# Late experts' blocks: partial sums kept in one PSUM bank and read while they grow

## The chip, the cores and the metric

The kernel runs on one core of a Trainium2 chip, as one program. The metric is its device time in microseconds (us), the median over runs; the profile is one further execution, taken with the hardware profiler.

## The reference: what is computed

An attention block without softmax (a state that decays at each step) makes `y` of shape batch 4, heads 8, 768 steps, 48 wide. Laid out as 3072 tokens of 384 numbers it goes into a mixture of 8 experts, two for each token:

```python
for t in range(S):
    state = f[:, :, t, :, None] * state + einsum('bhd,bhe->bhde', k[:, :, t], v[:, :, t])
    y[:, :, t] = einsum('bhd,bhde->bhe', q[:, :, t], state)
x = y.transpose(0, 2, 1, 3).reshape(3072, 384)
noisy = x @ w_gate + log1p(exp(x @ w_noise)) * noise
top2 = argpartition(-noisy, 2, axis=1)[:, :2]; top2_w = softmax over the two
for e in range(8):
    for k in range(2):
        mask = top2[:, k] == e
        h = maximum(x[mask] @ w1[e], 0.0)             # 384 -> 1024
        out[mask] += top2_w[mask, k, None] * (h @ w2[e])   # 1024 -> 384
```

All of it is in 32-bit floating point.

## The kernel before

**Stages.** First come attention and the routing, which write for each expert a list of its tokens; then the experts. A *pair* is 256 tokens of one list (two blocks of 128). An *item* is an expert with one to three pairs. Items 0 to 3 are early ones with one pair each; the twelve items end with eight *late* ones, 4 to 11, which take two or three pairs at once. `late_experts` sets their order: items 4, 5, 10 and 11 have two pairs (a *side* is then 256 tokens wide), items 6 to 9 have three (a side of 384). Tokens over 768 in a list are done in five blocks of 32, the *quarter* blocks, which are woven in among the pieces of items 6 to 10 (`quarter_block`, L1126 to L1161).

**Products saved.** A product of two matrices cut into 2 by 2 blocks is made here of seven block products and not eight: sums of blocks are made first (on VectorE), seven products are taken (on TensorE), and their results are combined. The first layer of a late item (`first_of_two`) does this for two of the three 128-row chunks of `x` and two sides of tokens: `a(half, chunk, j)` is a 128 by 128 block of `w1`, `b(chunk, side)` a chunk of the tokens' features turned round. Sums of `w1` are `s(1)` to `s(5)`, kept in `ws` (tile `v_all`), sums of `b` are `t(1)` to `t(4)`, kept in `ts` (tiles `v_all`, `f_all` and `qk_all`). The third chunk is multiplied plainly. A *group* `j` (four of them in an item) makes the hidden blocks `c(half, side)` of tile `hs_b`: eleven matmul calls of side width, each of which is two instructions in the trace. Calls and their order on TensorE: P1, X twice, P6, V twice, P7, Z twice, W twice, into seven PSUM banks.

The second layer of a pair (`second_layer`, one *call* for a pair, seven *pieces* with a `yield` behind each) does the same with halves of the 1024 hidden features, two blocks of tokens and two halves of the output's columns: seven products of four matmul calls, 192 columns wide. Its sums of hidden blocks are `sm[1]` to `sm[4]` (tile `f_all`, made by `inner_sums`), those of `w2` are `u[1]` to `u[4]` (tile `qk_all`, by `second_sums`). The result is scaled by the gate and added to the output in DRAM by GpSimd's indirect DMA (`scatter`).

**Order.** `in_order` ties each engine's instructions to the order in which the program's text issues them, so an instruction that waits holds up all behind it on its engine. Across engines there are only the waits that data and buffers need. Between the pieces `between` puts in the transposes of the next item's tokens (`turned`) and the sums for the next item's first layer (`first_sums`, L899). `one_bank` hands out the eight PSUM banks in turn. `ahead(1, ...)` and `ahead(2, ...)` put the loads of later weights on SP's queue.

Of the kernel before, what the change touches and what calls it, by code (L numbers as in the profile page):

```python
# [10 lines left out]
F32 = mybir.dt.float32  # L11
# [3 lines left out]
AF = mybir.ActivationFunctionType  # L15
AX = mybir.AxisListType
ALU = mybir.AluOpType
# [314 lines left out]
def kernel(  # L332
# [38 lines left out]
    nc = tc.nc  # L371
    B, H, S, D = q.shape
# [545 lines left out]
    def first_of_two(k):  # L918


        size = side_of(k)
        hs = wide[1][:, :, 0:2 * size]
        w = w1[home(k)]

        def a(half, chunk, j):
            return w[:, chunk, (half * FH + j) * 128:(half * FH + j + 1) * 128]

        def b(chunk, side):
            return (wide[0] if side else xt_a)[:, chunk, 0:size]

        def m(to, x, y, start, stop):
            nc.tensor.matmul(to, lhsT=x, rhs=y, start=start, stop=stop)  # L932

        def t(n):
            return ts[n][:, 0:size]

        for j in range(FH):
            def c(half, side):
                return hs[:, half * FH + j, side * size:(side + 1) * size]

            def s(n):
                return ws[n][:, j * 128:(j + 1) * 128]

            def bank(n):
                return one_bank(f"{n}{k}_{j}")[:, 0:size]

            def add(to, x, y):
                nc.vector.tensor_tensor(to, x, y, ALU.add)  # L948

            one, two, three, both = [kept(size) for _ in range(4)]  # L950
            P1, P6, V, P7, X, Z, W = bank("P1"), bank("P6"), bank("V"), bank("P7"), bank("X"), bank("Z"), bank("W")
            m(P1, a(0, 0, j), b(0, 0), True, True)
            nc.scalar.copy(one, P1)
            m(X, a(0, 1, j), b(1, 0), True, False)
            m(X, a(0, 2, j), b(2, 0), False, True)
            add(c(0, 0), one, X)
            nc.scalar.activation(c(0, 0), c(0, 0), AF.Relu)
            if j == FH - 1:
                inner_sums(hs, 3)
            m(P6, s(2), t(2), True, True)  # L960
            add(two, one, P6)
            m(V, s(1), t(1), True, False)
            m(V, a(1, 2, j), b(2, 1), False, True)
            add(both, two, V)
            m(P7, s(3), t(3), True, True)
            add(three, two, P7)
            add(c(1, 1), three, V)
            nc.scalar.activation(c(1, 1), c(1, 1), AF.Relu)  # L968
            if j < 2:
                second_sums(k, (3, 2)[j])  # L970
            yield
            m(Z, s(4), b(1, 1), True, False)
            m(Z, s(5), b(2, 1), False, True)
            add(c(0, 1), both, Z)
            nc.scalar.activation(c(0, 1), c(0, 1), AF.Relu)
            m(W, a(1, 1, j), t(4), True, False)
            m(W, a(1, 2, j), b(2, 0), False, True)
            add(c(1, 0), three, W)
            nc.scalar.activation(c(1, 0), c(1, 0), AF.Relu)
            if j < 2:  # L980
                second_sums(k, (1, 4)[j])
            if j == FH - 1:
                ahead(1, k + NR + 1)
            yield
        for q in range(len(items[k][1])):
            if q:
                inner_sums(hs[:, :, q * 256:], 3)
            yield from second_layer(k, first_of[k] + q, hs[:, :, q * 256:])

    def inner_sums(hs, which):  # L990
        def a(f, s):
# [3 lines left out]
                    3: (a(0, 0), a(0, 1), ALU.subtract), 4: (a(1, 0), sm[2], ALU.subtract)}[which]  # L995
        nc.vector.tensor_tensor(sm[which], x, y, op)  # L996

    def second_layer(k, p, hs):


        def a(f, s):
            return hs[:, f * FH:(f + 1) * FH, s * 128:(s + 1) * 128]

        def b(f, c):
            return w2[home(k)][:, f * FH:(f + 1) * FH, c * HC:(c + 1) * HC]

        bank, P = [], {}

        def product(name, x, y):
            if name not in (7, 5):  # L1010
                bank.append(one_bank(f"y{p}_{len(bank)}"))
            P[name] = bank[-1][:, HC:DM] if name in (7, 5) else bank[-1][:, 0:HC]
            for o in range(FH):
                nc.tensor.matmul(P[name], lhsT=x[:, o, :], rhs=y[:, o, :], start=(o == 0), stop=(o == FH - 1))  # L1014

        ys = [moved.tile([128, DM], F32, tag=f"ys{s}", name=f"ys{p}_{s}") for s in range(2)]
        P17 = ffn.tile([128, 2, HC], F32, tag="P17", name=f"P17_{p}", bufs=1)
        mid = ffn.tile([128, HC], F32, tag="mid", name=f"mid{p}", bufs=1)

        gate = [slots[p][:, s, 1:2].bitcast(F32) for s in range(2)]  # L1020

        def scatter(s):
            into = nc.gpsimd.indirect_dma_start(out=out, out_offset=bass.IndirectOffsetOnAxis(ap=slots[p][:, s, 2:3], axis=0),  # L1023
                                         in_=ys[s], in_offset=None, bounds_check=N - 1, oob_is_err=False, compute_op=ALU.add)
            tc.declare_no_dep(into.ins, group=f"pair{p}", reason="a list's tokens differ")
            tc.add_to_no_dep_group(f"pair{p}", into.ins)
            if p < NE:
                tc.declare_no_dep(into.ins, group="second half", reason="rows differ")
                tc.add_to_no_dep_group("first half", into.ins)


        calls = first_of[k + 1] - first_of[k]
        q = p - first_of[k]
        last = q == calls - 1
        turns_now, sums_now = {}, {}
        if k + 1 < len(items):
            to_turn = [(to, s) for to in range(first_of[k + 1], first_of[k + 2]) for s in range(2)]
            each = -(-len(to_turn) // calls)
            for piece, to in zip((1, 3) if each == 2 else (1, 2, 3) if each == 3 else (1, 2, 3, 4), to_turn[each * q:each * (q + 1)]):
                turns_now[piece] = [to]  # L1040
        if NE <= k + 1 < len(items):
            if q == 0:
                sums_now = {1: ["w1"], 2: ["w2"], 3: ["w3"], 4: ["w4"], 5: ["w5"]}
            if last:
                most = k + 1 > NE
                sums_now[4] = (["t1", "t2"] if most else []) + sums_now.get(4, [])
                sums_now[5] = (["t3", "t4"] if most else ["t1", "t2", "t3", "t4"]) + sums_now.get(5, [])

        def between(piece):
            for to in turns_now.get(piece, ()):  # L1050
                turned(*to)
            for which in sums_now.get(piece, ()):
                first_sums(k + 1, which)

        left, right = [y[:, 0:HC] for y in ys], [y[:, HC:] for y in ys]
        product(1, a(0, 0), b(0, 0))
        inner_sums(hs, 1)
        yield
        if k >= NE:
            between(1)  # L1060
        product(7, sm[3], u[3])
        nc.scalar.copy(P17.rearrange("t a w -> t (a w)"), bank[0][:, 0:DM])
        nc.scalar.mul(left[0], P17[:, 0], gate[0])
        if k < NE:
            between(1)
        inner_sums(hs, 2)
        yield
        product(4, a(1, 1), u[4])
        inner_sums(hs, 4)
        between(2)  # L1070
        yield
        product(5, sm[1], u[1])
        nc.vector.tensor_tensor(left[1], P17[:, 1], P[4], ALU.add)  # L1073
        nc.vector.tensor_tensor(right[1], P17[:, 1], P[5], ALU.add)
        between(3)
        yield
        product(6, sm[2], u[2])
        nc.vector.tensor_tensor(mid, P17[:, 0], P[6], ALU.add)
        for to in (left[1], right[1]):
            nc.vector.tensor_tensor(to, to, mid, ALU.add)  # L1080
        if p == NP - 1:
            nc.vector.tensor_scalar(ys[1], ys[1], gate[1], None, ALU.mult)
        else:
            nc.scalar.mul(ys[1], ys[1], gate[1])  # L1084
        scatter(1)
        nc.vector.tensor_tensor(mid, mid, P[5], ALU.add)
        nc.scalar.mul(right[0], mid, gate[0])
        between(4)
        yield
        product(2, a(1, 0), b(1, 0))  # L1090
        nc.vector.scalar_tensor_tensor(left[0], in0=P[2], scalar=gate[0], in1=left[0], op0=ALU.mult, op1=ALU.add)
        between(5)
        yield
        product(3, sm[4], b(1, 1))
        if last:
            ahead(2, k + NR + 1)
        nc.vector.scalar_tensor_tensor(right[0], in0=P[3], scalar=gate[0], in1=right[0], op0=ALU.mult, op1=ALU.add)
        scatter(0)
        if p == NP - 3:
            nc.gpsimd.drain()  # L1100
        between(6)
        yield
# [332 lines left out]
```

## Time and profile before

| | us |
|---|---|
| device time, median of 3 runs (range) | 647.41 (647.27 to 647.53) |
| the profiled execution: device time | 648.66 |
| its span, from the first to the last instruction | 646.9 |
| TensorE busy over the span | 635.9 (98%) |
| VectorE (DVE) busy | 443.2 (69%) |
| ScalarE (ACT) busy | 253.9 (39%) |
| GpSimd (POOL) busy | 270.8 (42%) |
| mean granted TensorE clock | 0.996 of full |

The profiled execution is 1.25 us above the median and 1.76 us above its own span. Of the engines TensorE is the fullest. In the profile a matmul's end is modelled, and the next one may start before it, so TensorE's busy share alone doesn't tell whether it waits; the starts of its rows do. PE is TensorE's matmuls and PEld its weight loads.

### The profile page before, as it was taken

Reading aid. Unit: us, or ns where it says so; the run is one execution under the profiler, and the core shown is the slowest. Engines: PE = TensorE matmul, PEld = TensorE weight load, DVE = VectorE, ACT = ScalarE, POOL = GpSimd, SP = SyncE. Lnnn points to the kernel's source line nnn. Section 1 sums busy time; section 2 is a strip of 40 time slices with the busy share of each in tenths; the row PEclk is TensorE's granted clock in tenths of the full one; section 3 lists DMA queues with packets and bytes.
Section 4 is the critical chain, followed back from the end, with each engine's and each line's share of the span. In section 5 each row is a group of like instructions: output and inputs, shape, how many; then the busy total and the mean of one; then the engine's idle time right before and its main releaser. Section 6 shows DMA issues by size and latency. Waiting matters only on the chain.

```text
span 646.9 us, 12901 instructions
## 1 busy us (share of the span) xinstructions
PE 635.9 (98%) x4883; PEld 549.7 (85%) x4883; DVE 443.2 (69%) x993; ACT 253.9 (39%) x602; POOL 270.8 (42%) x301
## 2 busy tenths in 40 slices
PE   8999999999999999999999999999999999999994
PEld 8999999888999999989758965995698579989994
DVE  6777878875656576677757575757566666767862
ACT  6976876752222233233332233323322332232330
POOL 7733899825476530352501460325034213503213
PEclk9999999999999999999999999999999999999998
DMA  9999888889998423368706560926093427622104
GB/s 186 195 224 206 175 166 161 180 213 289 293 246 205 75 42 103 55 193 297 194 27 241 108 186 10 310 38 195 11 311 68 124 88 235 134 64 26 23 1 55
DMA packets 153897, 96.31 MB, mean 149 GB/s; under 512 B 115600, under 2 KB 146320, under 8 KB 153824
## 3 DMA queue, kind: packets, MB, share of 16 engines
q1 hardware_dynamic: 141648, 76.12, 43.4%
q0 software_dynamic: 12176, 19.25, 15.4%
q8 instruction: 41, 0.67, 0.4%
q14 instruction: 32, 0.26, 0.1%
HBM read 75.97 MB, written 19.62 MB: 148 GB/s over the span
## 4 chain that ended last, share of the span: by engine, by line
PE 92%; DMA 3%; POOL 1%; ACT 1%; DVE 1%; SPq 0%; issue 0%; POOLq 0%; ACTq 0%
PE y L1014 34%; PE P L932 8%; PE hp L907 6%; PE X L932 5%; PE V L932 5%; PE Z L932 5%; PE W L932 5%; PE xp L626 3%; PE sc L573 3%; PE y L591 3%; DMA x_rows<-xs 3%; PE xgp L855 2%; PE y L602 1%; PE kp L533 1%; PE qp L533 1%; PE ds L597 1%
## 5 line engine op out<-in xcount | busy, mean ns | idle before, releaser
L1023 POOL DMA_INDIRECT out_dram<-ys,slots x48 | 81.0, 1687 | 160.1 <-ACT ys L1084 131.4
L1014 PE MATMUL y<-qk_all,f_all 128*128 128x192 f32 x576 | 105.3, 327 | 0.0
L1014 PEld LDWEIGHTS y<-qk_all,f_all 128*128 128x128 f32 x576 | 93.3, 190 | 0.4 <-DVE f_all L996 0.4
L819 POOL DMA_INDIRECT xg<-x_rows,slots x48 | 52.4, 1093 | 33.6 <-DMA slots<-lists 17.9
L1014 PE MATMUL y<-w,hs_b 128*128 128x192 f32 x320 | 59.1, 328 | 0.0
L703 POOL DMA_INDIRECT lists<-entry,sloti x48 | 54.6, 1138 | 10.4 <-issue 9.8
L1014 PEld LDWEIGHTS y<-w,hs_b 128*128 128x128 f32 x320 | 52.9, 190 | 0.9
L1160 POOL DMA_INDIRECT out_dram<-ys_q,slots_q x5 | 8.5, 1710 | 104.3 <-DVE ys_q L1158 104.3
L968 ACT ACTIVATE hs_b<-hs_b 128x256 f32<-128x256 f32 (+1 forms) x32 | 15.1, 470 | 71.4 <-DVE hs_b L948 71.4
L907 PE MATMUL hp<-xt_a,w 128*128 128x256 f32 x192 | 42.4, 380 | 0.0
L907 PEld LDWEIGHTS hp<-xt_a,w 128*128 128x128 f32 x192 | 36.2, 190 | 4.7
L932 PE MATMUL X<-xt_a,w 128*128 128x256 f32 (+1 forms) x128 | 39.7, 433 | 0.0
L932 PE MATMUL Z<-xt_b,v_all 128*128 128x256 f32 (+1 forms) x128 | 39.7, 433 | 0.0
L1073 DVE TENSOR_TENSOR ys<-P,y 128x192 f32<-128x192 f32 x24 | 8.5, 354 | 43.1 <-PE y L1014 30.0
L948 DVE TENSOR_TENSOR hs_b<-hs_a,X 128x256 f32<-128x256 f32 (+1 forms) x32 | 15.6, 487 | 30.6 <-PE X L932 30.1
L1084 ACT ACTIVATE ys<-ys,slots 128x384 f32<-128x384 f32 x23 | 14.1, 615 | 55.9 <-DVE ys L1080 55.9
L1014 PE MATMUL y<-w,f_all 128*128 128x192 f32 x192 | 35.2, 327 | 0.0
L576 DVE TENSOR_TENSOR A<-sc,causal 128x1024 f32<-128x1024 f32 x24 | 29.3, 1222 | 8.1 <-PE sc L573 8.0
L932 PEld LDWEIGHTS X<-xt_a,w 128*128 128x128 f32 x128 | 24.3, 190 | 10.1
L932 PEld LDWEIGHTS Z<-xt_b,v_all 128*128 128x128 f32 x128 | 24.3, 190 | 10.1
L948 DVE TENSOR_TENSOR hs_a<-hs_a,P 128x256 f32<-128x256 f32 (+1 forms) x64 | 31.1, 486 | 1.5
L1014 PEld LDWEIGHTS y<-w,f_all 128*128 128x128 f32 x192 | 31.8, 190 | 0.0
(200 smaller groups left out, 1439.4 us busy)
## 6 DMA issues: line engine op xcount, KB each, us to landing
w<-in_moe_w_dram SPq DMA_DIRECT2D x16, 1536.0 KB, 7.5
w_q<-in_moe_w_dram SPq DMA_DIRECT2D x10, 1536.0 KB, 10.0
w<-in_moe_w_dram SPq DMA_DIRECT2D x16, 384.0 KB, 6.1
f_all<-in_f_logit_dram SPq DMA_DIRECT2D x24, 192.0 KB, 3.0
qk_all<-in_q_dram SPq DMA_DIRECT2D x24, 192.0 KB, 5.5
qk_all<-in_k_dram SPq DMA_DIRECT2D x24, 192.0 KB, 4.5
v_all<-in_v_dram SPq DMA_DIRECT2D x24, 192.0 KB, 6.7
x_rows<-xs SPq DMA_DIRECT2D x24, 192.0 KB, 4.2
```

What stands on the lines that cost most here:

```text
L573: nc.tensor.matmul(sc[:, par, cols(hp)], lhsT=kQ[n][rows(par), cols(hp)], rhs=qP[n][rows(par), cols(hp)], start=True, stop=True)
L576: nc.vector.tensor_tensor(A[n].rearrange("j r (a i) -> j (r a) i", i=C), sc.rearrange("j r (a i) -> j (r a) i", i=C), causal.unsqueeze(1). ...
L591: nc.tensor.matmul(at(hp, par), lhsT=vt[:, 2 * hp + par, :], rhs=A[n][:, par, cols(hp)], start=(hp < 2), stop=(c == 0 and hp >= HP - 2))
L626: nc.tensor.matmul(xp[:, hp, :], lhsT=yT[n][:, hp % 2, cols(hp // 2)], rhs=w_rt[:, hp, :], start=True, stop=True)
L703: into = nc.gpsimd.indirect_dma_start(out=lists, out_offset=bass.IndirectOffsetOnAxis(ap=sloti[:, r, b:b + 1], axis=0), in_=entry[:, c, b, ...
L819: nc.gpsimd.indirect_dma_start(out=xg[p][:, s, :], out_offset=None, in_=x_rows[0:HALF * B * C] if p < NE else x_rows, in_offset=bass.Indir ...
L907: nc.tensor.matmul(hp[:, o, :], lhsT=w1[home(k)][:, i, (fo + o) * 128:(fo + o + 1) * 128], rhs=xt_a[:, i, k % 2 * 256:(k % 2 + 1) * 256], ...
L932: nc.tensor.matmul(to, lhsT=x, rhs=y, start=start, stop=stop)
L948: nc.vector.tensor_tensor(to, x, y, ALU.add)
L968: nc.scalar.activation(c(1, 1), c(1, 1), AF.Relu)
L1014: nc.tensor.matmul(P[name], lhsT=x[:, o, :], rhs=y[:, o, :], start=(o == 0), stop=(o == FH - 1))
L1023: into = nc.gpsimd.indirect_dma_start(out=out, out_offset=bass.IndirectOffsetOnAxis(ap=slots[p][:, s, 2:3], axis=0), in_=ys[s], in_offset= ...
```

## The change

Matmul calls stay the same in number and size; what moves is where they add up, who adds, and in which order they stand. Early items and their second layers are as before.

- **First layer of late items.** Three banks for a group and not seven. Bank A takes P1, P6, V and Z one after the other, bank B takes P7 and W, X stays alone. Between the calls ScalarE copies the partial sum out (`one` = P1, `two` = P1+P6, `seven` = P7). VectorE keeps three additions of the seven; c(0, 1) is read from bank A by ScalarE alone. Z (`sixth`) of a group moves behind the first two calls of the next group, and that of the last group behind the first product of the second layer.
- **Second layer of late items** (`late_second_layer`): X takes P1, P6, P5 and P3, Y takes P7 and P4, Z takes P2. ScalarE makes the first of each output quarter by a scaled copy, VectorE adds the rest with one fused operation each.
- **Sums sooner.** `sm[1]` to `sm[3]` are made in the last group, ahead of its last addition (`third`), and for the next pair of the same item at the fifth piece of this one.

In the diff `at_end` is the last group, `left_over` holds `sixth` of the group before (in the second layer's first call that of the last group, followed by `ahead(1, k + NR + 1)`, which before stood behind W), and `plus(to, bank, s)` is VectorE's `to += gate * bank`.

```diff
-            one, two, three, both = [kept(size) for _ in range(4)]
-            P1, P6, V, P7, X, Z, W = bank("P1"), bank("P6"), bank("V"), bank("P7"), ...
-            ...
+            def add(to, x, y):
+                nc.vector.tensor_tensor(to, x, y, ALU.add)
+                nc.scalar.activation(to, to, AF.Relu)
+            def first():
+                m(A, a(0, 0, j), b(0, 0), True, True)
+                nc.scalar.copy(one, A)
+            def fourth():
+                m(B, s(3), t(3), True, True)
+                nc.scalar.copy(seven, B)
+            def alone():
+                m(X, a(0, 1, j), b(1, 0), True, False)
+                m(X, a(0, 2, j), b(2, 0), False, True)
+                add(c(0, 0), one, X)
+            def second():
+                m(banks["A"], s(2), t(2), False, True, True)
+                nc.scalar.copy(two, banks["A"])
+            def seventh():
+                m(banks["B"], a(1, 1, j), t(4), False, False, True)
+                m(banks["B"], a(1, 2, j), b(2, 0), False, True, True)
+                add(c(1, 0), two, banks["B"])
+            def third():
+                m(banks["A"], s(1), t(1), False, False, True)
+                m(banks["A"], a(1, 2, j), b(2, 1), False, True, True)
+                add(c(1, 1), seven, banks["A"])
+            def sixth():
+                m(banks["A"], s(4), b(1, 1), False, False, True)
+                m(banks["A"], s(5), b(2, 1), False, True, True)
+                nc.scalar.activation(c(0, 1), banks["A"], AF.Relu)
...
+            first()
+            fourth()
+            for do in left_over:
+                do()
+            alone()
+            if j < 2:
+                second_sums(k, (3, 2)[j])
+            yield
+            second()
+            seventh()
+            if at_end:
+                for which in (1, 2, 3):
+                    inner_sums(hs, which)
+            third()
+            left_over = (sixth,)
+            if j < 2:
+                second_sums(k, (1, 4)[j])
+            yield
...
+    def late_second_layer(k, p, hs, left_over, next_hs):
+        product(X, a(0, 0), b(0, 0), start=True)
+        nc.scalar.mul(left[0], X, gate[0])
+        for do in left_over:
+            do()
+        yield
+        between(1)
+        product(Y, sm[3], u[3], start=True)
+        nc.scalar.mul(right[1], Y, gate[1])
+        yield
+        product(X, sm[2], u[2])
+        nc.scalar.mul(left[1], X, gate[1])
+        inner_sums(hs, 4)
+        between(2)
+        yield
+        product(Y, a(1, 1), u[4])
+        plus(left[1], Y, 1)
+        between(3)
+        yield
+        product(X, sm[1], u[1])
+        plus(right[1], X, 1)
+        scatter(1)
+        if next_hs is not None:
+            for which in (1, 2, 3):
+                inner_sums(next_hs, which)
+        between(4)
+        yield
+        product(Z, a(1, 0), b(1, 0), start=True)
+        plus(left[0], Z, 0)
+        between(5)
+        yield
+        product(X, sm[4], b(1, 1))
+        if last:
+            ahead(2, k + NR + 1)
+        nc.scalar.mul(right[0], X, gate[0])
+        scatter(0)
+        between(6)
+        yield
```

**TensorE, first group of item 4 and the start of the second.** Before (names as in the text; the number behind a name is the group):

```order
L932 MATMUL P_0_3376<-xt_a,w_1_146 128x256
L932 MATMUL X_0_3380<-xt_a,w_1_146 128x256 x2
L932 MATMUL P_0_3377<-f_all,v_all 128x256
L932 MATMUL V_0_3378<-v_all 128x256
L932 MATMUL V_0_3378<-xt_b,w_1_146 128x256
L932 MATMUL P_0_3379<-qk_all,v_all 128x256
L932 MATMUL Z_0_3381<-xt_b,v_all 128x256 x2
L932 MATMUL W_0_3382<-qk_all,w_1_146 128x256
L932 MATMUL W_0_3382<-xt_a,w_1_146 128x256
```

After:

```order
L932 MATMUL A_0_3376<-xt_a,w_1_146 128x256
L932 MATMUL B_0_3379<-qk_all,v_all 128x256
L932 MATMUL X_0_3382<-xt_a,w_1_146 128x256 x2
L932 MATMUL A_0_3376<-f_all,v_all 128x256
L932 MATMUL B_0_3379<-qk_all,w_1_146 128x256
L932 MATMUL B_0_3379<-xt_a,w_1_146 128x256
L932 MATMUL A_0_3376<-v_all 128x256
L932 MATMUL A_0_3376<-xt_b,w_1_146 128x256
L932 MATMUL A_1_3402<-xt_a,w_1_146 128x256
L932 MATMUL B_1_3405<-qk_all,v_all 128x256
L932 MATMUL A_0_3376<-xt_b,v_all 128x256 x2
```

P7 (`fourth`) now stands second, and bank A is written again (`second`) right behind X, and once more (`third`) three calls behind X.

**ScalarE, the same place.** After; L959, L964 and L974 copy `one`, `seven` and `two`, L951 are the Relus of `add`, L989 is the Relu of `sixth`:

```order
L959 COPY hs_a<-A_0_3376 128x256
L964 COPY hs_a<-B_0_3379 128x256
L951 ACTIVATE hs_b<-hs_b 128x256
L974 COPY hs_a<-A_0_3376 128x256
L951 ACTIVATE hs_b<-hs_b 128x256 x2
L959 COPY hs_a<-A_1_3402 128x256
```

The copy of `two` stands behind the Relu of c(0, 0), which itself needs VectorE's addition of X. Before, a group had one copy (L953) and four Relus (L957, L968, L975, L979) there.

**VectorE, last group of item 4.** Before, the last three additions of that group and what follows them (the sum `sm[3]`, made further up, is not shown):

```order
L948 TENSOR_TENSOR hs_b<-hs_a,V_3_3476 128x256
L948 TENSOR_TENSOR hs_b<-hs_a,Z_3_3479 128x256
L948 TENSOR_TENSOR hs_b<-hs_a,W_3_3480 128x256
L996 TENSOR_TENSOR f_all<-hs_b 128x512
L899 TENSOR_TENSOR v_all<-w_0_145 128x512
```

After:

```order
L950 TENSOR_TENSOR hs_b<-hs_a,X_3_3462 128x256
L950 TENSOR_TENSOR hs_b<-hs_a,B_3_3456 128x256
L1031 TENSOR_TENSOR f_all<-hs_b 128x512
L1031 TENSOR_TENSOR f_all<-f_all,hs_b 128x512
L1031 TENSOR_TENSOR f_all<-hs_b 128x512
L950 TENSOR_TENSOR hs_b<-hs_a,A_3_3453 128x256
```

Three sums over 512 columns now stand between the addition that reads bank B and the one that reads bank A.

More of the change, by code (lines that the diff above doesn't have):

```diff
@@ L929, in b, with m, group @@
             return (wide[0] if side else xt_a)[:, chunk, 0:size]
-        def m(to, x, y, start, stop):
-            nc.tensor.matmul(to, lhsT=x, rhs=y, start=start, stop=stop)
+        def m(to, x, y, start, stop, goes_on=False):
+            nc.tensor.matmul(to, lhsT=x, rhs=y, start=start, stop=stop, skip_group_check=goes_on)
         def t(n):
             return ts[n][:, 0:size]
-        for j in range(FH):
+        def group(j):
             def c(half, side):
@@ L948, in add @@
                 nc.vector.tensor_tensor(to, x, y, ALU.add)
-            one, two, three, both = [kept(size) for _ in range(4)]
[L951 to L968, printed above, removed]
+                nc.scalar.activation(to, to, AF.Relu)
+            one, two, seven = [kept(size) for _ in range(3)]
@@ new lines, in group @@
+            banks = {}
+            def first():
+                A = banks["A"] = bank("A")
+                m(A, a(0, 0, j), b(0, 0), True, True)
+                nc.scalar.copy(one, A)
+            def fourth():
+                B = banks["B"] = bank("B")
+                m(B, s(3), t(3), True, True)
+                nc.scalar.copy(seven, B)
+            def alone():
+                X = bank("X")
+                m(X, a(0, 1, j), b(1, 0), True, False)
+                m(X, a(0, 2, j), b(2, 0), False, True)
+                add(c(0, 0), one, X)
@@ new lines, in sixth @@
+            def sixth():
+                m(banks["A"], s(4), b(1, 1), False, False, True)
+                m(banks["A"], s(5), b(2, 1), False, True, True)
+                nc.scalar.activation(c(0, 1), banks["A"], AF.Relu)
+            return first, fourth, alone, second, seventh, third, sixth
+        left_over = ()
+        for j in range(FH):
+            first, fourth, alone, second, seventh, third, sixth = group(j)
+            at_end = j == FH - 1
+            first()
[3 more added lines that the diff above has]
+            alone()
@@ L971, in first_of_two, with sixth_of_last @@
             yield
[L972 to L979, printed above, removed]
+            second()
[5 more added lines that the diff above has]
+            left_over = (sixth,)
             if j < 2:
                 second_sums(k, (1, 4)[j])
-            if j == FH - 1:
-                ahead(1, k + NR + 1)
             yield
[L985 to L988, printed above, removed]
+        def sixth_of_last():
+            for do in left_over:
+                do()
+            ahead(1, k + NR + 1)
+        calls = len(items[k][1])
+        for q in range(calls):
+            yield from late_second_layer(k, first_of[k] + q, hs[:, :, q * 256:], () if q else (sixth_of_last,),
+                                         hs[:, :, (q + 1) * 256:] if q + 1 < calls else None)
     def inner_sums(hs, which):
@@ L996, in inner_sums, with second_parts @@
         nc.vector.tensor_tensor(sm[which], x, y, op)
-    def second_layer(k, p, hs):
-        def a(f, s):
-            return hs[:, f * FH:(f + 1) * FH, s * 128:(s + 1) * 128]
+    def second_parts(k, p):
         def b(f, c):
             return w2[home(k)][:, f * FH:(f + 1) * FH, c * HC:(c + 1) * HC]
[L1007 to L1014, printed above, removed]
         ys = [moved.tile([128, DM], F32, tag=f"ys{s}", name=f"ys{p}_{s}") for s in range(2)]
-        P17 = ffn.tile([128, 2, HC], F32, tag="P17", name=f"P17_{p}", bufs=1)
-        mid = ffn.tile([128, HC], F32, tag="mid", name=f"mid{p}", bufs=1)
         gate = [slots[p][:, s, 1:2].bitcast(F32) for s in range(2)]
@@ L1053, in between, with second_layer, a, product @@
                 first_sums(k + 1, which)
+        return b, ys, gate, scatter, last, between
+    def second_layer(k, p, hs):
+        def a(f, s):
+            return hs[:, f * FH:(f + 1) * FH, s * 128:(s + 1) * 128]
+        b, ys, gate, scatter, last, between = second_parts(k, p)
+        bank, P = [], {}
+        def product(name, x, y):
+            if name not in (7, 5):
+                bank.append(one_bank(f"y{p}_{len(bank)}"))
+            P[name] = bank[-1][:, HC:DM] if name in (7, 5) else bank[-1][:, 0:HC]
+            for o in range(FH):
+                nc.tensor.matmul(P[name], lhsT=x[:, o, :], rhs=y[:, o, :], start=(o == 0), stop=(o == FH - 1))
+        P17 = ffn.tile([128, 2, HC], F32, tag="P17", name=f"P17_{p}", bufs=1)
+        mid = ffn.tile([128, HC], F32, tag="mid", name=f"mid{p}", bufs=1)
         left, right = [y[:, 0:HC] for y in ys], [y[:, HC:] for y in ys]
@@ L1058, in second_layer @@
         yield
-        if k >= NE:
-            between(1)
         product(7, sm[3], u[3])
@@ L1063, in second_layer @@
         nc.scalar.mul(left[0], P17[:, 0], gate[0])
-        if k < NE:
-            between(1)
+        between(1)
         inner_sums(hs, 2)
@@ L1080, in second_layer @@
             nc.vector.tensor_tensor(to, to, mid, ALU.add)
[L1081 to L1084, printed above, removed]
+        nc.scalar.mul(ys[1], ys[1], gate[1])
         scatter(1)
@@ L1094, in second_layer, with a, product, plus @@
         product(3, sm[4], b(1, 1))
+        ahead(2, k + NR + 1)
+        nc.vector.scalar_tensor_tensor(right[0], in0=P[3], scalar=gate[0], in1=right[0], op0=ALU.mult, op1=ALU.add)
+        scatter(0)
+        between(6)
+        yield
+    def late_second_layer(k, p, hs, left_over, next_hs):
+        def a(f, s):
+            return hs[:, f * FH:(f + 1) * FH, s * 128:(s + 1) * 128]
+        b, ys, gate, scatter, last, between = second_parts(k, p)
+        X, Y, Z = (one_bank(f"y{p}_{i}")[:, 0:HC] for i in range(3))
+        def product(to, x, y, start=False):
+            for o in range(FH):
+                nc.tensor.matmul(to, lhsT=x[:, o, :], rhs=y[:, o, :], start=(start and o == 0), stop=(o == FH - 1),
+                                 skip_group_check=not start)
+        left, right = [y[:, 0:HC] for y in ys], [y[:, HC:] for y in ys]
+        def plus(to, bank, s):
+            nc.vector.scalar_tensor_tensor(to, in0=bank, scalar=gate[s], in1=to, op0=ALU.mult, op1=ALU.add)
+        product(X, a(0, 0), b(0, 0), start=True)
+        nc.scalar.mul(left[0], X, gate[0])
+        for do in left_over:
+            do()
+        yield
+        between(1)
+        product(Y, sm[3], u[3], start=True)
[23 more added lines that the diff above has]
+        product(X, sm[4], b(1, 1))
         if last:
             ahead(2, k + NR + 1)
-        nc.vector.scalar_tensor_tensor(right[0], in0=P[3], scalar=gate[0], in1=right[0], op0=ALU.mult, op1=ALU.add)
+        nc.scalar.mul(right[0], X, gate[0])
         scatter(0)
```

## The prediction

> **What bounds the kernel now.** I read the page first, then the busy time by stretches, then the timeline of the late items, and last the queues of POOL and SP. From the page, and from the stretch in which the late items run (columns: PE, PEld, DVE, ACT, POOL busy us, clock, DMA share, GB/s):
>
> ```profile
> span 646.9 us, 12901 instructions
> PE 635.9 (98%) x4883; PEld 549.7 (85%) x4883; DVE 443.2 (69%) x993; ACT 253.9 (39%) x602; POOL 270.8 (42%) x301
> 232.00:638.50 406.50, 406.50 (x2417) 340.38 (x2415) 278.52 (x592) 129.85 (x288) 122.21 (x87) 1.00 0.45 124
> ```
>
> From 232 to 638.5 us PE is busy without a break, at the full clock. Since ends of matmuls are modelled, I look at starts. The timeline of a group of item 4 (side 256; columns: start, us, engine, line, what, instructions, idle before):
>
> ```profile
> 244.73 1.03 PE L932 MATMUL X<-xt_a,w 128*128 128x256 f32 x4
> 244.96 0.42 ACT L979 ACTIVATE hs_b<-hs_b 128x256 f32<-128x256 f32 x1 [0.45 <-DVE hs_b L948]
> 245.28 0.35 ACT L953 COPY hs_a<-P 128x256 f32<-128x256 f32 x1
> 245.60 0.59 PE L932 MATMUL P<-f_all,v_all 128*128 128x256 f32 x2
> 245.87 0.42 DVE L948 TENSOR_TENSOR hs_b<-hs_a,X 128x256 f32<-128x256 f32 x1 [0.94 <-PE X L932]
> 246.32 0.42 ACT L957 ACTIVATE hs_b<-hs_b 128x256 f32<-128x256 f32 x1 [0.69 <-DVE hs_b L948]
> 246.89 0.59 PE L932 MATMUL P<-qk_all,v_all 128*128 128x256 f32 x2
> ```
>
> Four instructions of X take 0.87 (244.73 to 245.60), the six of P6 and V 1.29 (to 246.89): 0.215 us each, bank changes or not. So there is no gap between the calls that DVE, ACT or a bank could have made, and a call of this width costs 0.43. The matmul calls are the same after the change, so work taken off DVE buys nothing here; what counts is each new wait in PE's queue. A call of side 384 costs 0.645, by the rows further down.
>
> The Trainium skill, "Perfetto Trace Analysis", section Identifying the Most-Contended Engine, speaks against this reading: matmul busy share is no measure of headroom, and the share of weight loading is to be used. By it PEld's 340.38 of 406.50 would leave up to 66 us inside PE, of which a relieved DVE could win a part, and the sum below would begin from a gain. The starts disagree (six instructions in 1.29, none late), and the measurement decides: the sum begins from nothing.
>
> **First layer, the wait of `third`.** Let T be the moment when X of a group has streamed (245.60 above). Bank A is written by `second` right away, and by `third` three calls later, T + 1.29. In between ACT must have copied `two` out of it. That copy stands behind the Relu of c(0, 0), and this behind DVE's addition of X: addition at T + 0.27, Relu at T + 0.72 (246.32). A copy starts 0.32 after a Relu ahead of it (244.96, 245.28) and takes 0.35: it ends at T + 1.39. How a held PE goes on is seen where the second layer now waits for a sum:
>
> ```profile
> 621.33 0.69 DVE L996 TENSOR_TENSOR f_all<-hs_b 128x512 f32<-128x512 f32 x1 [0.48 <-ACT hs_b L979]
> 622.06 0.69 DVE L996 TENSOR_TENSOR f_all<-f_all,hs_b 128x512 f32<-128x512 f32 x1
> ...
> 629.23 1.46 PE L1014 MATMUL y<-w,hs_b 128*128 128x192 f32 x8
> 629.88 1.30 DVE L996 TENSOR_TENSOR f_all<-hs_b 128x512 f32<-128x512 f32 x2
> 630.63 1.27 PEld L1014 LDWEIGHTS y<-qk_all,f_all 128*128 128x128 f32 x8 [0.24 <-DVE f_all L996]
> 630.63 1.57 PE L1014 MATMUL y<-qk_all,f_all 128*128 128x192 f32 x8
> ```
>
> The first of the two sums ends at 630.57; the weight load starts 0.06 later, and the eight matmuls take 1.57 where they take 1.46 when the weights were loaded ahead: 0.17 from release to streaming. I take the same from ACT to PE. So `third` streams at T + 1.56 and not T + 1.29: 0.27 lost in each group. Items 4, 5, 10 and 11 have 16 such groups: **4.3 us**. What is queued behind: everything of PE. Bounds, over all 16: nothing, if the chain is 0.3 shorter; 5.6, if it is 0.08 longer.
>
> Side 384, with the same steps:
>
> ```profile
> 392.67 0.55 DVE L948 TENSOR_TENSOR hs_b<-hs_a,X 128x384 f32<-128x384 f32 x1 [2.21 <-PE X L932]
> 393.05 0.81 PE L932 MATMUL V<-v_all 128*128 128x384 f32 x2
> 393.26 0.52 ACT L957 ACTIVATE hs_b<-hs_b 128x384 f32<-128x384 f32 x1 [1.47 <-DVE hs_b L948]
> 394.98 1.45 PE L932 MATMUL Z<-xt_b,v_all 128*128 128x384 f32 x4
> 398.43 1.45 PE L932 MATMUL X<-xt_a,w 128*128 128x384 f32 x4
> 399.03 0.48 ACT L953 COPY hs_a<-P 128x384 f32<-128x384 f32 x1
> 399.72 0.49 PE L932 MATMUL P<-f_all,v_all 128*128 128x384 f32 x1
> 399.99 0.56 DVE L948 TENSOR_TENSOR hs_b<-hs_a,X 128x384 f32<-128x384 f32 x1 [1.67 <-PE X L932]
> ```
>
> Addition at T + 0.27 (399.72 to 399.99), Relu 0.59 later, copy 0.42 after that (0.52 less the overlap of 0.10 at 256), 0.48 for the copy, 0.17: T + 1.93. Three calls take 1.93 (393.05 to 394.98). So it just fits: **0**, at most 0.11 (the weight load laid bare) in 16 groups, 1.8.
>
> The other waits of a group are covered. `one` and `seven` are copied four calls or more ahead of the next write (1.7 us against a copy of 0.35). `sixth` needs bank A free 0.86 after `third` has streamed; DVE's addition ends 0.27 + 0.42 after it, and 0.17 make just 0.86: nothing, at most 0.11 in 12 groups (1.3). The sums of `w2` stand behind it on DVE; at side 384 a call is longer and leaves 0.3.
>
> **First layer's end, the wait of `sixth`.** In the last group DVE makes three sums between the addition from bank B and that from bank A. Side 256: B has streamed at T + 1.29, addition 1.56 to 1.98, Relu 2.01 to 2.43, first sum at 2.46, the second 0.73 later (it needs the first: 621.33, 622.06), the third and the addition 0.61 apart (two sums in 1.30), addition 4.41 to 4.83, PE released to stream at T + 5.00. PE: `third` from 1.56 to 2.42, then the second layer's first product, 1.30 (635.94 to 637.24 below). It arrives at 3.72 and loses 1.28. In items 6 to 10 the last piece of a quarter block stands between and covers it:
>
> ```profile
> 404.97 1.53 PE L1154 MATMUL yp_q<-w_q,hts_q 128*32 128x96 f32 x64
> 406.43 1.57 PE L1014 MATMUL y<-w,hs_b 128*128 128x192 f32 x8
> ```
>
> That piece is 1.46. Item 10 arrives at 5.18: nothing lost. Side 384 arrives at 1.93 + 1.29 + 1.46 + 1.30 = 5.98, released at 6.01 by the same chain with its durations: 0.03 in four items. Left are items 4, 5 and 11: 3 x 1.28 + 0.1 = **3.9 us**; bounds 3.0 and 6.8 (0.3 to either side in each of three, and 0.5 in each of four items of 384).
>
> **The start of item 4.** P7 moved from seventh to second call, and needs t3:
>
> ```profile
> 235.24 1.03 PE L932 MATMUL X<-xt_a,w 128*128 128x256 f32 x4
> 235.34 0.42 DVE L899 TENSOR_TENSOR qk_all<-xt_b 128x256 f32<-128x256 f32 x1
> ```
>
> `fourth` arrives where X stood, 235.24; t3 is done at 235.76, streams at 235.93: **0.7 us**, once (0.4 to 0.9). In later items t1 and t2 stand one piece sooner, and behind the sixth product DVE has one addition, t3 and t4: t3 is ready before the seventh has streamed.
>
> **Second layer.** Sums 1 to 3 are made early, so the waits of 0.21 as at 630.63 go (0.10 late, 0.11 weight load; two such in the run): **-0.4**. In the new order each bank is read for one product (1.30) before it is written again, and the reader needs 0.27 + 0.45 + 0.17: covered, whether DVE or ACT reads.
>
> **The end.**
>
> ```profile
> L1063 ACT ACTIVATE ys<-P,slots 128x192 f32<-128x192 f32 x20 | 9.1, 455 | 0.7
> 635.94 1.46 PE L1014 MATMUL y<-w,hs_b 128*128 128x192 f32 x8
> 637.24 1.46 PE L1014 MATMUL y<-w,f_all 128*128 128x192 f32 x8
> 637.89 1.55 POOL L1023 DMA_INDIRECT out_dram<-ys,slots  x1 [5.28 <-DVE mid L1086]
> 638.81 0.42 DVE L1097 SCALAR_TENSOR_TENSOR ys<-y,slots,ys 128x192 f32<-128x192 f32 x1 [0.61 <-PE y L1014]
> 639.75 1.56 POOL L1023 DMA_INDIRECT out_dram<-ys,slots  x1 [0.30 <-issue]
> ```
>
> The last scatter waits for the scatter ahead of it (637.89 + 1.55 + 0.31). That one is now ready after one operation behind the fifth product (635.94 + 0.27 + 0.42), and the last then follows its own scaled copy: 638.54 + 0.27 + 0.45 + 0.3 = 639.56. **-0.2**.
>
> **Sum.** 4.3 + 3.9 + 0.7 - 0.4 - 0.2 = +8.3. The profiled span would be 655.2; this execution (648.66) lay 1.25 above the median, to which I add the same: 647.41 + 8.3 = 655.7.
>
> **Rivals.**
>
> *Not slower: PE goes on past a waiting call.* Were the calls behind a held one (other banks, data at hand) to run meanwhile, both waits would vanish, and what is left is 0.7 - 0.6: 647.5. The point from which it decides: calls of the next group start ahead of `third`. The row at 630.63 speaks against it: PE and its loads both stood. The same time results if the chain to `two` is under 1.12 and the sums let the addition go first, which the code's order excludes.
>
> *Faster: hidden gaps.* If 0.05 us at each of the 32 groups and 20 calls of the second layer were a wait on DVE that no row names, its relief would win 2.6, and `third` would have to cost nothing: 647.41 - 2.6 - 0.6 + 0.7 = 644.9. The even starts speak against it. This is where the Trainium skill's rule above would lead.
>
> *Much slower: SP and POOL.* `ahead(1)` now waits for `sixth`, 2.8 us later, and the lists of the quarter block stand behind it on SP, their gather on POOL, the scatters behind that:
>
> ```profile
> 405.07 0.37 SPq L827 DMA_DIRECT2D w<-in_moe_w_dram  x1
> 413.21 1.10 POOL L1116 DMA_INDIRECT xg_q<-x_rows,slots_q  x1 [3.31 <-DMA slots_q<-lists]
> 417.94 1.87 POOL L1023 DMA_INDIRECT out_dram<-ys,slots  x1 [0.39 <-DVE f_all L996]
> out_dram<-ys,slots POOLq DMA_INDIRECT x48, 4.7
> ```
>
> The gather goes from 413.2 to 416.0, the first call's second scatter from 417.9 to about 419.3, landing at 424. ACT writes that buffer again in the third call near 427.2 (two calls of 9.7 behind 406.43, one product more). Landing over 3 us late would hold ACT and then PE, 1 to 3 us in four items: 660 to 668.
>
> **How the numbers follow.** The forecast has 0.80; not slower 0.09; faster 0.05; much slower 0.06. Bounds of the terms: 4.3 can be 1.8 (only weight loads laid bare) to 5.6, side 384 up to 1.8, side 256 ahead of `sixth` up to 1.3, 3.9 from 3.0 to 6.8, 0.7 from 0.4 to 0.9, less 0.6: +4.6 to +15.8, which is 652.0 to 663.2. They don't all lie high together; 651.2 to 661.0 holds the forecast nearly whole and nothing of the first two rivals. This kernel's runs can tell a change of about 0.2% (1.3 us) from none: faster 0.05, same 0.09, slower 0.86.
>
> **What would show it.** Idle time of PEld on A in the first layer, released by ACT's copy (L974), some 0.27 in each group of side 256 and about none at 384; idle of 1.2 to 1.4 ahead of `sixth` in items 4, 5 and 11, released by DVE (L950); one wait of 0.7 on t3; none for `sm` sums. DVE's busy time falls and ACT's rises without a gain. I am wrong if PE still runs unbroken through the late items, or if other waits (banks of the second layer, scatters) carry the loss.

## The result, and the profile after

The changed kernel took 656.92 us (median; 655.91 to 658.15), and the kernel before, run beside it, 647.47 (647.27 to 647.96). The ratio is 1.0146, with a 95% interval of 1.0127 to 1.0164: 1.5% slower. The prediction said 655.7 (651.2 to 661.0), and 655.2 for the span. The page of the profile after begins so:

```profile
span 655.4 us, 12756 instructions
PE 640.7 (98%) x4883; PEld 547.1 (83%) x4883; DVE 353.8 (54%) x764; ACT 270.8 (41%) x667; POOL 266.6 (41%) x301
```

DVE was relieved of 89 us (443.2 to 353.8) and ACT took on 17, and the kernel is slower. To see where, I cut each trace at two points that every version has: the start of the first matmul of item 4 and the start of the last matmul of the program. The same 2398 matmuls start in this *late part*. Before, and then after (columns as in the row of stretches above):

```profile
234.80:638.37 403.57, 403.57 (x2398) 337.55 (x2397) 276.00 (x586) 128.53 (x285) 121.30 (x87) 1.00 0.45 125
```

```profile
234.39:646.67 412.28, 408.75 (x2398) 334.94 (x2397) 187.09 (x358) 145.13 (x349) 118.00 (x87) 1.00 0.45 122
```

The late part became 8.71 us longer at the same full clock. Item 4 began 0.41 sooner, and behind the last matmul's start 0.16 more was needed; that makes the 8.5 of the two spans. Who was waited for in the late part stands in the views of waits of PEld and of PE (us in total, times, longest):

```profile
PEld A L932 <- ACT hs_a L974: 11.8, 32, 0.7
PEld A L932 <- DVE hs_b L950: 3.9, 3, 1.3
```

```profile
PE B L932 <- DVE qk_all L899: 0.5, 1, 0.5
```

These are the three waits of the prediction: `third` on ACT's copy of `two`, `sixth` on DVE, `fourth` on t3. The totals are idle times of the weight loads, and part of that lies beside matmuls that still run: what TensorE lost has to be read from starts. Of the 11.8, 5.5 stand in the 16 groups of side 384 (0.34 each), for which the prediction had about none; by the starts all but one of these groups lost nothing. A group of item 4, the second:

```profile
241.88 0.59 PE L932 MATMUL A<-f_all,v_all 128*128 128x256 f32 x2
...
242.15 0.42 DVE L950 TENSOR_TENSOR hs_b<-hs_a,X 128x256 f32<-128x256 f32 x1 [2.24 <-PE X L932]
...
242.60 0.42 ACT L951 ACTIVATE hs_b<-hs_b 128x256 f32<-128x256 f32 x1 [1.01 <-DVE hs_b L950]
242.74 0.59 PE L932 MATMUL B<-xt_a,w 128*128 128x256 f32 x2
242.92 0.35 ACT L974 COPY hs_a<-A 128x256 f32<-128x256 f32 x1
243.33 0.30 PEld L932 LDWEIGHTS A<-v_all 128*128 128x128 f32 x2 [0.40 <-ACT hs_a L974]
243.33 0.70 PE L932 MATMUL A<-v_all 128*128 128x256 f32 x2
...
243.87 0.38 PE L932 MATMUL A<-xt_b,w 128*128 128x256 f32 x1
```

T is 241.88. Addition at T + 0.27, Relu at T + 0.72, the copy from T + 1.04 to T + 1.39, weights 0.06 later. From `seventh`'s second call (242.74) to `third`'s second (243.87) are 1.13 where two calls take 0.86: 0.27 lost. And the end of item 4, where DVE's three sums stand ahead of the addition that reads bank A:

```profile
254.32 1.46 PE L1147 MATMUL y<-w,hs_b 128*128 128x192 f32 x8
254.37 0.69 DVE L1031 TENSOR_TENSOR f_all<-hs_b 128x512 f32<-128x512 f32 x1 [0.48 <-ACT hs_b L951]
254.52 0.37 SPq L827 DMA_DIRECT2D w<-in_moe_w_dram  x1
...
255.10 0.69 DVE L1031 TENSOR_TENSOR f_all<-f_all,hs_b 128x512 f32<-128x512 f32 x1
255.71 0.68 DVE L1031 TENSOR_TENSOR f_all<-hs_b 128x512 f32<-128x512 f32 x1
256.31 0.41 DVE L950 TENSOR_TENSOR hs_b<-hs_a,A 128x256 f32<-128x256 f32 x1
...
256.77 0.73 PEld L932 LDWEIGHTS A<-xt_b,v_all 128*128 128x128 f32 x4 [1.28 <-DVE hs_b L950]
256.78 1.13 PE L932 MATMUL A<-xt_b,v_all 128*128 128x256 f32 x4 [0.99 <-DVE hs_b L950]
```

By the even starts the product's last matmul has streamed at 255.62 (254.32 + 1.30), and `sixth` starts at 256.78; with 0.10 for its weight load laid bare it loses 1.26.

### The profile page after: what moved, and what is told of

Same layout as the page of the kernel before. It is cut to its first block, busy times and chain, and to the rows that moved or that the text cites. A ratio compares the mean times of both kernels' runs of the same rounds, so it can differ in the third digit from the quotient of the medians.

```text
span 655.4 us, 12756 instructions
## 1 busy us (share of the span) xinstructions
PE 640.7 (98%) x4883; PEld 547.1 (83%) x4883; DVE 353.8 (54%) x764; ACT 270.8 (41%) x667; POOL 266.6 (41%) x301
## 3 DMA queue, kind: packets, MB, share of 16 engines
q0 software_dynamic: 12176, 19.25, 15.6%
## 5 line engine op out<-in xcount | busy, mean ns | idle before, releaser
L951 ACT ACTIVATE hs_b<-hs_b 128x256 f32<-128x256 f32 (+1 forms) x96 | 45.1, 470 | 102.2 <-DVE hs_b L950 102.2
L1147 PE MATMUL y<-qk_all,f_all 128*128 128x192 f32 x480 | 84.6, 326 | 0.0
L1147 PEld LDWEIGHTS y<-qk_all,f_all 128*128 128x128 f32 x480 | 77.4, 190 | 0.1
L1153 DVE SCALAR_TENSOR_TENSOR ys<-y,slots,ys 128x192 f32<-128x192 f32 x60 | 24.9, 415 | 96.1 <-ACT ys L1165 45.0
L950 DVE TENSOR_TENSOR hs_b<-hs_a,X 128x256 f32<-128x256 f32 (+1 forms) x32 | 15.6, 488 | 83.2 <-PE X L932 83.2
L932 PE MATMUL A<-xt_b,v_all 128*128 128x256 f32 (+1 forms) x128 | 40.0, 435 | 3.0 <-DVE hs_b L950 3.0
L1188 ACT ACTIVATE ys<-y,slots 128x192 f32<-128x192 f32 x20 | 8.4, 421 | 72.5 <-PE y L1147 72.5
L932 PEld LDWEIGHTS A<-xt_b,v_all 128*128 128x128 f32 x128 | 23.9, 190 | 12.8 <-DVE hs_b L950 3.9
L547 DVE TENSOR_TENSOR_SCAN L<-f,cap 128x512 f32<-128x512 f32 x24 | 29.6, 1235 | 1.0 <-ACT cap L542 1.0
L1031 DVE TENSOR_TENSOR f_all<-hs_b 128x512 f32<-128x512 f32 x40 | 27.4, 685 | 4.3 <-ACT hs_b L951 4.3
L1147 PE MATMUL y<-qk_all,hs_b 128*128 128x192 f32 x160 | 29.3, 326 | 0.0
```

The lines of the kernel that those rows point to most:

```text
L547: nc.vector.tensor_tensor_scan(L[n], data0=logf[n], data1=cap[n % 2].rearrange("d a t -> d (a t)"), initial=0.0, op0=ALU.add, op1=ALU.min)
L932: nc.tensor.matmul(to, lhsT=x, rhs=y, start=start, stop=stop, skip_group_check=goes_on)
L951: nc.scalar.activation(to, to, AF.Relu)
L1147: nc.tensor.matmul(to, lhsT=x[:, o, :], rhs=y[:, o, :], start=(start and o == 0), stop=(o == FH - 1), skip_group_check=not start)
L1153: nc.vector.scalar_tensor_tensor(to, in0=bank, scalar=gate[s], in1=to, op0=ALU.mult, op1=ALU.add)
```

## The experiments

My theory: TensorE is the bound, and the change only put three waits into its queue, each with a price that the order of ACT's and DVE's instructions sets. The rivals of the prediction remain as rivals here: another bound (the second layer, SP, POOL), or a wait that could be taken away without winning anything. Times were taken in two sets on two chips. In the second set the part ahead of item 4 took 9 to 15 us longer (the last section shows it), so its times are read by their ratios and by the late part. The late part is that of each kernel's one profiled execution.

| kernel | us, median | ratio to before (95%) | late part |
|---|---|---|---|
| before, beside the changed one | 647.47 | 1 | 403.57 |
| after | 656.92 | 1.0146 (1.0127 to 1.0164) | 412.28 |
| before, first set | 647.19 | 1 | |
| ACT's copy first | 652.20 | 1.0073 (1.0059 to 1.0088) | 408.51 |
| sums behind `third` | 652.79 | 1.0088 (1.0073 to 1.0102) | 409.49 |
| t3 first | 655.56 | 1.0136 (1.0121 to 1.0151) | 411.78 |
| all three | 646.70 | 0.9998 (0.9987 to 1.0009) | 403.21 |
| before, second set | 658.99 | 1 | |
| second layer alone | 659.82 | 0.9998 (0.9969 to 1.0026) | 403.46 |
| Relu twice | 684.10 | 1.0359 (1.0296 to 1.0422) | 427.52 |
| loads a piece sooner | 668.80 | 1.0116 (1.0052 to 1.0179) | 412.27 |

**ACT's copy first.** The Relu of c(0, 0) goes behind the copy of `two`.

```diff
 def alone():
     ...
-    add(c(0, 0), one, X)
+    nc.vector.tensor_tensor(c(0, 0), one, X, ALU.add)
 def second():
     m(banks["A"], s(2), t(2), False, True, True)
     nc.scalar.copy(two, banks["A"])
+    nc.scalar.activation(c(0, 0), c(0, 0), AF.Relu)
```

> Edit to the changed kernel: ScalarE copies `two` out of bank A ahead of the Relu of c(0, 0) and not behind it. Theory (the copy stands too late in ScalarE's queue): `second` has streamed 0.43 behind X, the copy runs from 0.70 to 1.05, TensorE is released at 1.22 and arrives at 1.29, so the 0.27 in each of the 16 groups of side 256 and the one 0.33 at side 384 go, 4.6 us. `sixth` of items 4, 5 and 11 is then reached 0.27 sooner while VectorE's sums end as before, so its wait grows from 1.26 to 1.53: 0.8 back. 656.9 - 3.8 = 653.1. Rival (writing a bank again that has just been read costs by itself, whatever the order of the readers): the waits on bank A stay, 656.9.

Measured 652.20; the late part is 3.77 shorter than after's. The same place of the second group of item 4, now with T = 239.86:

```profile
239.86 0.59 PE L932 MATMUL A<-f_all,v_all 128*128 128x256 f32 x2
...
240.49 0.37 ACT L974 COPY hs_a<-A 128x256 f32<-128x256 f32 x1 [0.91 <-PE A L932]
240.72 0.59 PE L932 MATMUL B<-xt_a,w 128*128 128x256 f32 x2
240.76 0.42 ACT L975 ACTIVATE hs_b<-hs_b 128x256 f32<-128x256 f32 x1
241.15 0.59 PE L932 MATMUL A<-v_all 128*128 128x256 f32 x2
```

The copy begins 0.20 after the call it reads has streamed and ends 0.29 ahead of `third`, which now follows at 0.43 like any other call. All waits on the copy are gone. Not all of their price is won, for `sixth` waits longer:

```profile
PEld A L932 <- DVE hs_b L950: 4.6, 3, 1.5
```

DVE's three sums end when they did, counted from X, and TensorE arrives 0.27 sooner: by the starts `sixth` loses 1.52 instead of 1.26, 0.8 in three items. Two waits on one chain are not worth their sum.

**Sums behind `third`.** DVE makes the three sums after the addition that reads bank A.

```diff
+            third()
             if at_end:
                 for which in (1, 2, 3):
                     inner_sums(hs, which)
-            third()
```

> Edit to the changed kernel: in the last group the three sums stand behind `third` on VectorE. Theory (the sums hold up the addition that frees bank A for `sixth`): the three waits of 1.26 go, 3.8 us. The third sum, which the product into bank Y needs, then ends 5.05 behind X where TensorE arrives at 4.91 (items 4 and 5) or 4.58 (item 11, no transposes there): with 0.17 for release 0.3 twice and 0.6 once come back, 1.3 us. 656.9 - 3.8 + 1.3 = 654.4. Rival (`sixth` waits for its place behind the first product and not for the sums): 656.9.

Measured 652.79, late part 2.79 shorter than after's. The end of item 4:

```profile
252.54 1.46 PE L1147 MATMUL y<-w,hs_b 128*128 128x192 f32 x8
252.74 0.42 DVE L950 TENSOR_TENSOR hs_b<-hs_a,A 128x256 f32<-128x256 f32 x1 [0.64 <-PE A L932]
...
253.84 1.03 PE L932 MATMUL A<-xt_b,v_all 128*128 128x256 f32 x4
254.41 0.68 DVE L1031 TENSOR_TENSOR f_all<-hs_b 128x512 f32<-128x512 f32 x1
255.15 1.92 PEld L1147 LDWEIGHTS y<-qk_all,f_all 128*128 128x128 f32 x12 [0.19 <-DVE f_all L1031]
```

`sixth` follows the product without a gap (252.54 + 1.30 = 253.84); the 3.79 are won whole. The second product now waits for `sm[3]`, the third of the sums (254.41 + 0.68, then the load): 0.22 in items 4 and 5, where transposes stand between, and 0.55 in item 11, together 1.0. 412.28 - 3.79 + 1.0 = 409.49, which is what the late part shows.

**t3 first.** Item 4's sums of features are made in another order.

```diff
-["t1", "t2", "t3", "t4"]
+["t3", "t1", "t2", "t4"]
```

> Edit to the changed kernel: for item 4 alone VectorE makes t3 ahead of t1 and t2. Theory: the one wait of 0.75 at the start of item 4 goes, 656.2, and no row of TensorE waits for qk_all there. That is near what the times can tell; the profile's row decides. Rival (that wait is for a bank or for the tokens' transposes): the row stays.

Measured 655.56, late part 0.50 shorter. In the changed kernel `fourth` started 1.10 behind the start of item 4 (234.39), where one call takes 0.43; with its weight load partly laid bare that is 0.75 lost:

```profile
235.49 0.67 PE L932 MATMUL B<-qk_all,v_all 128*128 128x256 f32 x2 [0.51 <-DVE qk_all L899]
```

With t3 first it follows its predecessor without a gap:

```profile
233.09 0.59 PE L932 MATMUL A<-xt_a,w 128*128 128x256 f32 x2
233.53 0.59 PE L932 MATMUL B<-qk_all,v_all 128*128 128x256 f32 x2
...
235.35 0.41 DVE L950 TENSOR_TENSOR hs_b<-hs_a,X 128x256 f32<-128x256 f32 x1
```

The wait of 0.75 is gone, and 0.25 of it comes back, which was not expected: DVE's remaining sums hold up the addition of X (T + 0.53 instead of T + 0.27), and the wait of `third` in this one group grows by that.

**All three.** The edits above together, with the sums in the order 3, 1, 2, since the second product reads `sm[3]`.

> Edit to the changed kernel: the copy first, t3 first, and the three sums behind `third` in the order 3, 1, 2. Theory: all three kinds of wait go and none comes in their place (sum 3 ends at 3.4 behind X, needed at 4.3; sum 2 at 4.8, needed at 5.6), so TensorE runs unbroken but for the quarter blocks. Left is what the change gave: 0.4 for the sums of the second layer and 0.2 at the end. 647.5 - 0.6 = 646.9, a ratio of 0.999 to the kernel before; no idle row on A. Rival (accumulating in a bank that is read in between costs something that no wait shows): above 649.

Measured 646.70, ratio 0.9998 (0.9987 to 1.0009): the loss is gone, and nothing is won. The late part (first row) and its longest waits of PEld:

```profile
235.36:638.57 403.21, 403.21 (x2398) 337.29 (x2397) 187.23 (x358) 145.74 (x349) 121.75 (x87) 1.00 0.46 125
```

```profile
PEld xgp_q L1224 <- issue: 2.5, 5, 0.5
PEld yp_q L1246 <- issue: 2.5, 5, 0.5
PEld hp_q L1231 <- DVE hs_b L950: 2.5, 5, 0.5
PEld A L932 <- issue: 2.1, 5, 0.4
```

No wait on a copy, a sum or t3 is left; the rows shown are where TensorE passes to and from the quarter blocks, and the changed kernel has them too. DVE works 89 us less in the late part than before the change (276.00 to 187.23), and the late part is 0.36 shorter. That is the two small waits of the second layer that went (0.21 and 0.15 before). Between the calls no wait is left that these edits could take away.

**Second layer alone.** The first layer as before the change, with its seven banks and seven additions, and the new second layer behind it. Against the kernel before, the first layer differs by this:

```diff
             if j == FH - 1:
+                for which in (1, 2):
+                    inner_sums(hs, which)
                 ahead(1, k + NR + 1)
```

> The kernel before with the second layer of the change alone: first layer in seven banks as before, then the new second layer with sums 1 and 2 made right behind the last group (sum 3 was made there before already). Theory (the loss is all in the first layer and its end): 647.5 - 0.4 - 0.2, with 0.2 back in item 11, where sum 2 is needed 0.2 before it is done: 647.1. Rival (the second layer's banks, each read between two products, cost a part of the 9.4 us): 649 or more.

Ratio 0.9998 (0.9969 to 1.0026), which alone says no more than within 0.3%. The late part says it closer: 403.46, 0.11 less than before. The two small waits of before, 0.36 together, are gone, and by the starts one of 0.24 came in item 11, ahead of the product that reads `sm[2]`:

```profile
634.88 0.69 DVE L998 TENSOR_TENSOR f_all<-f_all,hs_b 128x512 f32<-128x512 f32 x1
...
635.69 1.27 PEld L1114 LDWEIGHTS y<-qk_all,f_all 128*128 128x128 f32 x8 [0.27 <-issue]
```

The row names no releaser; that it is `sm[2]`, ready at 635.57, is read from the times and from the 0.2 expected there. Otherwise TensorE runs as before. The second layer's banks, read in between, cost nothing that this shows; the loss is in the first layer and its end.

**Relu twice.** Each group gets one more instruction on ACT ahead of the copy of `two`.

```diff
     add(c(0, 0), one, X)
+    nc.scalar.activation(c(0, 0), c(0, 0), AF.Relu)
```

> Edit to the changed kernel: the Relu of c(0, 0) stands twice on ScalarE (the values stay the same), which makes the chain to the copy of `two` longer by one Relu's step, 0.32 at side 256 and 0.42 at side 384. Theory (the chain just fits at 384 and is 0.27 too long at 256): every one of the 32 groups pays all of it, 16 x 0.32 + 16 x 0.42 = 11.8; the end of items 4, 5 and 11 gives 0.4 back, since `sixth` arrives later. 656.9 + 11.4 = 668.3. Rival (side 384 has room to spare, which is why it shows no waits): 5.1 - 0.4, 661.6.

Ratio 1.0359 (1.0296 to 1.0422), which holds the expected 1.032. The late part grew by 15.24, not by the 11.4 that 668.3 stands for. A group of side 256 and one of side 384:

```profile
252.90 0.42 ACT L951 ACTIVATE hs_b<-hs_b 128x256 f32<-128x256 f32 x1 [1.00 <-issue]
253.04 0.59 PE L932 MATMUL B<-xt_a,w 128*128 128x256 f32 x2
253.35 0.42 ACT L971 ACTIVATE hs_b<-hs_b 128x256 f32<-128x256 f32 x1
253.67 0.35 ACT L975 COPY hs_a<-A 128x256 f32<-128x256 f32 x1
...
254.61 0.59 PE L932 MATMUL A<-xt_b,w 128*128 128x256 f32 x2
...
405.96 0.52 ACT L951 ACTIVATE hs_b<-hs_b 128x384 f32<-128x384 f32 x1 [1.46 <-DVE hs_b L950]
...
406.39 0.81 PE L932 MATMUL B<-xt_a,w 128*128 128x384 f32 x2
406.51 0.52 ACT L971 ACTIVATE hs_b<-hs_b 128x384 f32<-128x384 f32 x1
...
408.20 0.81 PE L932 MATMUL A<-xt_b,w 128*128 128x384 f32 x2
```

Side 256: 1.57 where two calls take 0.86, so 0.71 lost instead of 0.27, more by 0.45: the whole of the added instruction. Side 384: 1.81 where two calls take 1.29, so 0.52 to 0.53, where nothing was lost. With 16 groups of each that makes 15.6, less the 0.4 by which `sixth` waits shorter. What the expectation had too small is the step of the added Relu. It took that of a copy behind a Relu (0.32 and 0.42); the second Relu, which reads what the first writes, starts 0.45 behind it at side 256 (252.90, 253.35) and 0.55 at side 384 (405.96, 406.51). That side 384 pays nearly all of it holds: of 0.55 it loses 0.52 to 0.53, so the chain there ends about 0.03 before TensorE arrives.

**Loads a piece sooner.** `ahead(1)` is issued in the last group, as before the change, not behind `sixth`.

```diff
+            if at_end:
+                ahead(1, k + NR + 1)
             yield
 def sixth_of_last():
     for do in left_over:
         do()
-    ahead(1, k + NR + 1)
```

> Edit to the changed kernel: the load of the next but one item's first weights goes back on SP's queue behind the last group, ahead of `sixth` (which reads no such weights). Theory (SP, POOL and the scatters are hidden): the scatters of the first calls move up by 1 to 3 us and the time stays, 656.9 (656.2 to 657.6). Rival (a part of the loss comes from scatters that land late): 1 us or more less.

The interval of the ratio (1.0052 to 1.0179) does not tell the two theories apart. The late part is the same as after's: 412.27 against 412.28. SP's load that `ahead(1)` issues at the end of item 7, of after and then of this kernel:

```profile
409.06 0.37 SPq L827 DMA_DIRECT2D w<-in_moe_w_dram  x1
```

```profile
420.71 0.37 SPq L827 DMA_DIRECT2D w<-in_moe_w_dram  x1
```

Counted from the start of item 4 (234.39, and 246.04 here) the load comes at 174.67 in both. The text's order is not what held it, and the expected shift of 1 to 3 us did not happen. So this run says nothing of late scatters; "all three" does, where the loss is gone though `ahead(1)` still stands behind `sixth`.

## Why the prediction was right

By its own steps, each against the starts of the matmuls after:

- **`third`, 4.3.** It lost 0.265 in each of the 16 groups of side 256, 4.24, by the very chain: T + 0.27, 0.72, 1.39, and 0.17 from there to the stream (0.06, and the weight load laid bare, 0.11). The 0.17, taken from a release by DVE, held for one by ACT. With the copy moved ahead, the waits went; with a Relu more, they grew by that Relu.
- **Side 384, 0.** It lost nothing in 15 groups and 0.32 in one, in item 7. That lies inside the bound of 1.8, but not for the bound's reason: there the addition of X came late, which the prediction did not have (last section).
- **`sixth`, 3.9.** It lost 3 x 1.263 = 3.79, in items 4, 5 and 11 and nowhere else; the quarter blocks' pieces covered the other five items as said. The sums' order was the cause: with the addition first, all of it was won.
- **t3, 0.7.** It was 0.75, and with t3 made first it went.
- **The sums' waits, -0.4.** Both are gone: 0.36.
- **The end, -0.2: not won, and too small to matter.** The last scatter is issued sooner behind the last matmul's start (647.73 against 646.67, where before it was 639.75 against 638.37: 0.32 less), as forecast. But what follows it took 0.5 longer, so the end came 0.16 later. The end lies 8.72 behind the last matmul's start here, 8.64 to 9.55 in the seven traces of the experiments, and 8.56 in the one trace of before; whether the change lengthened it, one trace of before does not tell.

```profile
647.73 1.55 POOL L1043 DMA_INDIRECT out_dram<-ys,slots  x1 [1.05 <-ACT ys L1188]
```

4.56 + 3.79 + 0.75 - 0.36 = 8.74, against 8.71 in the late part. The medians differ by 9.45, 0.7 more than this. In the two profiled executions the rest of the program took 0.25 less after the change, not more, so the late part does not account for the 0.7, and the runs do not explain it. On the first set's chip the time by the late part alone would be 647.19 + 8.71 = 655.9; no run shows it.

**The rivals.** *PE goes on past a waiting call:* no. In the group shown no matmul into another bank started between 242.74's two matmuls and `third`, and taking the three waits away won everything back. *Hidden gaps:* no. Both "all three" and "second layer alone" relieve DVE (by 89 and 31 us of the late part's 276.00) and leave TensorE's late part within 0.4 us. The Trainium skill, "Perfetto Trace Analysis", section Identifying the Most-Contended Engine, has TensorE's headroom judged by the busy share of the weight loads, beside the share of the peak's arithmetic that is reached. That busy time is 337.29 of 403.21 with all three edits, as good as before (337.55 of 403.57), and no more than 0.4 us of the 66 was won by relieving DVE. So the traces disagree with it as far as a relief of DVE goes; other ways to win from the 66 us were not tried. *SP and POOL:* its premise was wrong. I said that the loads wait for `sixth`; in item 4 the load starts at 254.52, 0.2 behind `third`, while `sixth` starts at 256.78. The position in the text binds an engine's own instructions, and SP's only to SP's; by the text the last reader of the load's buffer is `third`, and `sixth` reads other tiles. The sum did not rest on it.

## What to carry to other kernels

In this kernel one engine's starts were without a gap, and 89 us of work taken off another won nothing but two small waits, 0.36 together. What had to be counted is each place where the full engine must now wait: follow that chain through the *order* of the instructions on the helping engine, not through its busy time. Reading an accumulating bank in between was free here once the reader's copy stood first in its engine's queue and ended before the next write; one Relu ahead of the copy cost 4 us, and three sums ahead of an addition another 4. Where waits hang on one chain, taking one away can lengthen the next (0.8 of 4.6 us came back here), so try removing them together.

## What the runs showed of the hardware

Two things were not expected. In all seven kernels with the new first layer, the addition of X in the third group of item 7 began 0.62 after X had streamed, and not 0.27, with DVE idle ahead of it; in five of them this costs TensorE 0.32 to 0.35, and nothing where the copy stands first.

```profile
398.00 0.81 PE L932 MATMUL A<-f_all,v_all 128*128 128x384 f32 x2
398.63 0.55 DVE L950 TENSOR_TENSOR hs_b<-hs_a,X 128x384 f32<-128x384 f32 x1 [4.50 <-PE X L932]
```

It is always at that place, so it belongs to the program and not to the run; what it is, no row names.

And the part ahead of item 4 was not the same in the second set, which was taken on another chip. There item 4 began at 244 to 248 us where it began at 233 to 235 elsewhere. At 150 to 180 us the granted clock was 0.78, 0.94 and 0.88 in its three traces, against 1.00 in the others; the lowest is "second layer alone":

```profile
150.00:180.00 30.00, 27.16 (x158) 22.17 (x156) 12.10 (x38) 6.52 (x15) 8.74 (x14) 0.78 0.72 216
```

TensorE was also less busy there, and fewer bytes were moved (216 GB/s, against 297 before the change). Which came first, and whether it is the chip or the moment, was not tried. The late parts of that set do not show it: the loads a piece sooner gave 412.27 against 412.28 for after.
